# Dividing by the softmax sums with scaled copies on ScalarE in the first two blocks of a fused attention and two-layer kernel

## The chip, the cores and the metric

The kernel runs on one core of a Trainium2 chip. A core has five engines with a queue each: TensorE (PE: matrix products and transposes), VectorE (DVE), ScalarE (ACT), GpSimd (POOL) and SyncE (SP, which here issues the transfers between memory and the core). The metric is the device time of one execution in microseconds; the value given is the median of several runs.

## The reference

For 4 batch items and 8 heads of width 64, each of 512 local queries attends to the keys within 32 positions and to 32 global keys; 32 global queries attend to everything. The result, reordered to 2176 rows of 512, goes through two feed-forward parts.

```python
s_ll = np.where(np.abs(pos[:, None] - pos[None, :]) <= 32, scale * q_l @ k_l.T, -1e9)
s_l = np.concatenate([scale * q_l @ k_g.T, s_ll], axis=-1)
e = np.exp(s_l - max(s_l)); a_l = e / (sum(e) + 1e-09)
out_l = a_l @ concat(v_g, v_l)            # out_g likewise, without the mask
x = concat(out_g, out_l) as (2176, 512)
h = x @ w_in                              # 512 -> 2048
x = where(h > 0, h, exp(min(h, 0)) - 1) @ w_out
xn = x / sqrt(mean(x * x) + 1e-6) * rms_g
out = (silu(xn @ w_gate) * (xn @ w_val)) @ w_o2   # 512 -> 1536 -> 512
```

## The kernel before, in words

The local queries are cut into 16 units of 128 queries, u = 0 to 15, four to a batch item. A unit has all 8 heads, in two halves (`par`) of four. It goes through five helpers. `a_S` makes the scores s of both halves in PSUM on TensorE. `a_E` takes the maximum of each row on VectorE (L227), scales it (L228), and makes the exponentials E on ScalarE, one instruction of 128x128 for each head (L230). `a_T` transposes E on TensorE and copies it out as ET on ScalarE (L238). `a_PV` multiplies by the values; a column of ones among these gives the sum of each row as column 64 of o (L249). `a_N` adds 1e-9 to the sums (L262), inverts them (L263) and multiplies o by the result into x (L264), all on VectorE. `a_X` transposes four units' x and splits them into two parts, xT: a cast on ScalarE (L273) and the rest on VectorE (L274).

Four units make a block of 512 tokens for the first feed-forward part. Block b runs over 16 slices j of the inner width: `mm1` makes h (12 matmuls, L130), `act1` makes the activation tile g in two parts (a cast on ScalarE, L137, and the rest on VectorE, L138), and `mm2` adds g's product to four accumulators y (12 matmuls, L144), one slice later. In block b the units of block b+1 are worked on in between (`att_slot`): scores at j = 0, 4, 8, 12, transposes one slice later, values two slices later.

The weights arrive as raw 64-bit words and are decoded on the way. A tile of 128x1024 takes an absolute value on ScalarE (dx, L81), two one-input passes on VectorE (L88, L89), two two-input passes (L90, L91), a cast on ScalarE (wA, L94) and a subtraction on VectorE (L97). The first layer's 16 tiles are decoded in the prologue (tiles 0 to 2) and in block 0 (one per slice); the last feed-forward part's tiles later.

The prologue (units 0 to 3) has its order written out by hand for TensorE, VectorE and ScalarE (L384 to L433). From block 0 on only TensorE's order is the written one; that of VectorE, ScalarE and SyncE is set by a scheduler at build time, which knows the dependences and its own estimates of durations. Each engine then runs its list strictly in order.

Of the kernel before, what the change touches and what calls it, by code (L numbers as in the profile page):

```python
# [11 lines left out]
AF = mybir.ActivationFunctionType  # L12
ALU = mybir.AluOpType
# [7 lines left out]
P = 128  # L21
# [4 lines left out]
SCALE = 0.125  # L26
# [15 lines left out]
def fused_kernel(ctx: ExitStack, tc: tile.TileContext, kq, vl, gkq, gv, w_in, w_out, w_gate, w_val, w_o2, rms_g, consts, out):  # L42
    nc = tc.nc
# [103 lines left out]
    def new_y():  # L147
        return [yps.tile([P, 512], F32, tag=f"y{i}", name=f"y{i}") for i in range(4)]
# [26 lines left out]
    with ExitStack() as ls:  # L175
# [46 lines left out]
        def a_E(u):  # L222
            ss = s_t.pop(u)
            mx = small.tile([P, 2, 4], F32, tag="st", name="mx")
            e = [ap_.tile([P, 4, P], F32, tag=f"E{par}", name="E") for par in range(2)]
            for par in range(2):
                nc.vector.tensor_reduce(out=mx[:, par, :], in_=ss[par], axis=AX.X, op=ALU.max)  # L227
                nc.vector.tensor_scalar(out=mx[:, par, :], in0=mx[:, par, :], scalar1=-SCALE, scalar2=None, op0=ALU.mult)  # L228
                for pr in range(4):
                    nc.scalar.activation(e[par][:, pr, :], ss[par][:, pr, :], AF.Exp, bias=mx[:, par, pr:pr + 1], scale=SCALE)  # L230
            e_t[u] = e
# [21 lines left out]
        def a_N(u):  # L253
            b, T = u // 4, u % 4
            if T == 0:
                x_t[b] = moe.tile([P, 4, 512], F32, tag="x32", name="x")
            x = x_t[b][:, T, :].rearrange("p (a e d) -> p e a d", a=4, e=2)
            os_ = o_t.pop(u)
            st = small.tile([P, 2, 4, 2], F32, tag="st", name="st")
            for par in range(2):  # L260
                o = os_[par]
                nc.vector.tensor_scalar(out=st[:, par, :, 0:1], in0=o[:, :, 64:65], scalar1=1e-9, scalar2=None, op0=ALU.add)  # L262
                nc.vector.reciprocal(st[:, par, :, 1:2], st[:, par, :, 0:1])  # L263
                nc.vector.tensor_tensor(out=x[:, par], in0=o[:, :, 0:64], in1=st[:, par, :, 1:2].to_broadcast([P, 4, 64]), op=ALU.mult)  # L264

        def a_X(b, cs, xT, pools):

# [11 lines left out]
        def att_slot(b, j, part):  # L279

            u, jj = 4 * (b + 1) + j // 4, j % 4
            if jj == 0 and part == 0:
                a_S(u, ATT2)
                a_E(u)
                load_kq(u + 1)
            if jj == 1 and part == 1:
                a_T(u, 0, aps, "att")
                a_T(u, 1, aps, "att")
            if jj == 2 and part == 0:
                a_PV(u, ATT2)  # L290
                a_N(u)
                load_v(u + 1)
# [91 lines left out]
        with tc.manual_schedule(engines={mybir.EngineType.DVE, mybir.EngineType.Activation}):  # L384
# [11 lines left out]
            a_S(0, ATT2)  # L396
            w1_bits(0)
            a_E(0)
            a_S(1, HB)
            a_T(0, 0, yps, "y0")  # L400
            a_T(0, 1, yps, "y1")
            w1_hi(0)
            a_E(1)
            a_PV(0, Y2)
            w1_lo(0)
            a_N(0)
            w1_abs(1)
            a_S(2, ATT2)
# [3 lines left out]
            w1_bits(1)  # L412
            a_PV(1, Y2)
            a_N(1)
            a_S(3, HB)
            a_T(2, 0, yps, "y0")
# [375 lines left out]
    for k in range(5):  # L792
        n = sizes[k] * P
        xn = xn_t.pop(k)
        os_ = new_y()
# [118 lines left out]
```

## Time and profile before

| what | us |
|---|---|
| median of 3 runs | 933.08 |
| range of the runs | 931.52 to 933.91 |
| profiled execution | 932.09 |
| its span in the profile | 930.0 |
| TensorE busy in the span | 900.3 |
| VectorE busy | 457.9 |
| ScalarE busy | 346.3 |

The span is from the first to the last instruction. Busy times of a whole span are averages over stages: here a prologue, blocks 0 to 3 of the first feed-forward part (block 0 starts at 40.69, block 1 at 150.63, block 2 at 255.17), and the last part. Matmuls overlap, so their rows are longer than the distance from one to the next. The same holds for rows of VectorE and ScalarE: the price of an instruction in a full queue is the distance to the start of the next.

### The profile page before, as it was taken

The numbers are of one execution on the slowest core, as the hardware profiler recorded it, in microseconds if no ns is written. First come the engines' busy times: TensorE is split into PE (matmuls) and PEld (weight loads), VectorE is DVE, ScalarE is ACT, GpSimd is POOL, SyncE is SP. The second block draws the span as 40 slices with busy tenths as digits, with TensorE's granted clock in tenths as the row PEclk, the third lists the DMA queues.
The fourth block names the chain that finished last, engine by engine and source line by source line (L and its number), as shares of the span: only waits on it lengthen the run. The fifth ranks groups of instructions, "written<-read, shape, count | busy, mean of one in ns | idle before, by whom it ended". The sixth has DMA issues, their size and how long they took to land.

```text
span 930.0 us, 15199 instructions
## 1 busy us (share of the span) xinstructions
PE 900.3 (97%) x6482; PEld 752.6 (81%) x6482; DVE 457.9 (49%) x791; ACT 346.3 (37%) x627; POOL 17.9 (2%) x19
## 2 busy tenths in 40 slices
PE   5789999999999999999999999999999999999997
PEld 3567778888878887767888888888889999999996
DVE  4899965676687875443875115221422142142111
ACT  4677754434444433333756113212312232232111
POOL 0000000000000000000101000001000100100000
PEclk8999999999999999999999999999999999999999
DMA  9686443455576743532644001100100010000000
GB/s 360 268 300 214 158 178 123 166 181 195 213 275 219 281 160 137 176 137 90 228 126 144 1 1 35 45 1 1 35 20 27 1 34 35 1 1 35 1 1 35
DMA packets 34443, 107.74 MB, mean 116 GB/s; under 512 B 3016, under 2 KB 5704, under 8 KB 31816
## 3 DMA queue, kind: packets, MB, share of 16 engines
q1 hardware_dynamic: 34376, 106.77, 32.2%
q8 instruction: 51, 0.84, 0.4%
q14 instruction: 16, 0.13, 0.0%
HBM read 88.41 MB, written 18.35 MB: 115 GB/s over the span
## 4 chain that ended last, share of the span: by engine, by line
PE 87%; DVE 7%; issue 2%; DMA 2%; ACT 2%; SPq 0%; ACTq 0%; DVEq 0%
PE y L144 17%; PE h L130 16%; PE pg L631 15%; PE pv L631 15%; PE y L637 15%; PE o L249 2%; DVE dx L90 1%; PE ptp L236 1%; PE yg L595 1%; PE hg L579 1%; PE s L218 1%; DVE dx L91 1%; DVE wA L97 1%; DMA raw<-in_moe_w_in 1%; DVE dx L88 1%
## 5 line engine op out<-in xcount | busy, mean ns | idle before, releaser
L144 PE MATMUL y<-g,wA 128*128 128x512 f32 x768 | 199.0, 402 | 6.3 <-DVE g L138 4.5
L130 PE MATMUL h<-xT,wA 128*128 128x512 f32 x768 | 186.4, 392 | 1.3 <-DVE xT L274 1.3
L144 PEld LDWEIGHTS y<-g,wA 128*128 128x128 f32 x768 | 140.7, 190 | 42.4 <-DVE g L138 6.4
L130 PEld LDWEIGHTS h<-xT,wA 128*128 128x128 f32 x768 | 144.0, 189 | 32.3 <-DVE xT L274 1.5
L804 DVE TENSOR_TENSOR silu<-pv,silu 128x384 f32<-128x384 f32 (+1 forms) x60 | 36.6, 611 | 257.2 <-PE pv L631 251.2
L637 PE MATMUL y<-wB,p 128*128 128x512 f32 x612 | 149.0, 391 | 0.0
L637 PEld LDWEIGHTS y<-wB,p 128*128 128x128 f32 x612 | 114.4, 188 | 22.4
L803 ACT ACTIVATE silu<-pg 128x384 f32<-128x384 f32 (+1 forms) x60 | 32.1, 534 | 159.5 <-PE pg L631 159.4
L631 PE MATMUL pv<-xT,wB 128*128 128x384 f32 (+1 forms) x432 | 88.4, 352 | 0.0
L631 PEld LDWEIGHTS pv<-xT,wB 128*128 128x128 f32 x432 | 77.3, 188 | 5.6
L806 ACT CAST p<-silu 128x384 fp32r<-128x384 f32 (+1 forms) x60 | 33.3, 555 | 127.0 <-DVE silu L804 126.8
L137 ACT CAST g<-e 128x512 fp32r<-128x512 f32 x64 | 39.7, 621 | 64.9 <-DVE e L113 61.1
L111 ACT ACTIVATE e<-h 128x512 f32<-128x512 f32 x48 | 28.9, 602 | 92.5 <-PE h L130 86.6
L631 PE MATMUL pv<-xnB,wB 128*128 128x512 f32 (+1 forms) x288 | 61.5, 362 | 0.0
L631 PE MATMUL pg<-xT,wB 128*128 128x384 f32 (+1 forms) x288 | 60.0, 357 | 0.0
L631 PEld LDWEIGHTS pg<-xT,wB 128*128 128x128 f32 x288 | 52.2, 188 | 5.8 <-issue 0.5
L631 PEld LDWEIGHTS pv<-xnB,wB 128*128 128x128 f32 x288 | 52.2, 188 | 5.6
L807 DVE TENSOR_TENSOR p<-silu,p 128x384 fp32r<-128x384 f32 (+1 forms) x60 | 38.0, 633 | 35.5 <-ACT p L806 35.5
L112 DVE TENSOR_SCALAR e<-e 128x512 f32<-128x512 f32 x52 | 22.2, 427 | 64.6 <-ACT e L111 64.3
L138 DVE TENSOR_TENSOR g<-e,g 128x512 fp32r<-128x512 f32 x64 | 45.0, 703 | 15.3 <-ACT g L137 14.4
L81 ACT ACTIVATE dx<-raw 128x1024 f32<-128x1024 f32 x34 | 39.1, 1151 | 12.3 <-DVE wA L97 6.1
L90 DVE SCALAR_TENSOR_TENSOR dx<-raw,dx 128x1024 int32<-128x1024 int32 x34 | 42.0, 1239 | 0.6
(153 smaller groups left out, 911.1 us busy)
## 6 DMA issues: line engine op xcount, KB each, us to landing
raw<-in_moe_w_out SPq DMA_DIRECT2D x14, 1024.0 KB, 5.7
wT<-dx SPq DMA_DIRECT2D x18, 512.0 KB, 3.3
wraw<-wT SPq DMA_DIRECT2D x18, 512.0 KB, 4.4
raw<-in_moe_w_in SPq DMA_DIRECT2D x8, 1024.0 KB, 8.7
raw<-in_moe_w_gate SPq DMA_DIRECT2D x6, 1024.0 KB, 6.4
raw<-in_moe_w_val SPq DMA_DIRECT2D x6, 1024.0 KB, 6.9
gvr<-in_gv SPq DMA_DIRECT2D x8, 640.0 KB, 4.8
gkq<-in_gkq SPq DMA_DIRECT2D x4, 1152.0 KB, 5.2
```

The source lines that it names most:

```text
L81: ins = nc.scalar.activation(x, f(words(raw)[:, :, 1]), AF.Abs)
L90: nc.vector.scalar_tensor_tensor(out=i32(x), in0=word[:, :, 1], scalar=-0x40000000, in1=i32(x), op0=ALU.bitwise_and, op1=ALU.bitwise_or)
L130: nc.tensor.matmul(h[:, :n], W1[c, G][:, ws, o:o + P], xT[c][:, xs, :n], start=(k == 0), stop=(k == 11))
L137: nc.scalar.copy(g[:, 0, :n], e[:, :n])
L138: nc.vector.tensor_tensor(out=g[:, 1, :n], in0=e[:, :n], in1=f(g[:, 0, :n]), op=ALU.subtract)
L144: nc.tensor.matmul(ys[dc][:, :n], W2[j][:, ws, dc * P:(dc + 1) * P], g[:, gs, :n], start=(j == 0 and k == 0), stop=(j == 15 and k == 2))
L631: nc.tensor.matmul(ps[:, :n], W[c, G3][:, ws, o:o + P], xn[c][:, xs, :n], start=(k == 0), stop=(k == 11))
L637: nc.tensor.matmul(os_[t], p[:, pp, t * P:(t + 1) * P], Wo[j][:, ww, :], start=(j == 0 and k == 0), stop=(j == 11 and k == 2))
L803: nc.scalar.activation(s[:, :n], pg[:, :n], AF.Silu)
L804: nc.vector.tensor_tensor(out=s[:, :n], in0=pv[:, :n], in1=s[:, :n], op=ALU.mult)
L806: nc.scalar.copy(p[:, 0, :n], s[:, :n])
L807: nc.vector.tensor_tensor(out=p[:, 1, :n], in0=s[:, :n], in1=f(p[:, 0, :n]), op=ALU.subtract)
```

## The change

In `a_E` the maxima of both halves are scaled by one instruction on 128x8, after both reductions, instead of by one on 128x4 after each. In `a_N` the reciprocals of both halves are joined in the same way. For units 0 to 7 (the prologue's four, and the four that are worked on in block 0) the product on VectorE is replaced by eight copies on ScalarE, one for each head, of 128x64, with the reciprocal as the per-partition scale.

```diff
             for par in range(2):
                 nc.vector.tensor_reduce(out=mx[:, par, :], in_=ss[par], axis=AX.X, op=ALU.max)
-                nc.vector.tensor_scalar(out=mx[:, par, :], in0=mx[:, par, :], scalar1=-SCALE, scalar2=None, op0=ALU.mult)
+            nc.vector.tensor_scalar(out=mx, in0=mx, scalar1=-SCALE, scalar2=None, op0=ALU.mult)
+            for par in range(2):
                 for pr in range(4):
                     nc.scalar.activation(e[par][:, pr, :], ss[par][:, pr, :], AF.Exp, bias=mx[:, par, pr:pr + 1], scale=SCALE)
...
             for par in range(2):
+                nc.vector.tensor_scalar(out=st[:, par, :, 0:1], in0=os_[par][:, :, 64:65], scalar1=1e-9, scalar2=None, op0=ALU.add)
+            nc.vector.reciprocal(st[:, :, :, 1:2], st[:, :, :, 0:1])
+            for par in range(2):
                 o = os_[par]
-                nc.vector.tensor_scalar(out=st[:, par, :, 0:1], in0=o[:, :, 64:65], scalar1=1e-9, scalar2=None, op0=ALU.add)
-                nc.vector.reciprocal(st[:, par, :, 1:2], st[:, par, :, 0:1])
-                nc.vector.tensor_tensor(out=x[:, par], in0=o[:, :, 0:64], in1=st[:, par, :, 1:2].to_broadcast([P, 4, 64]), op=ALU.mult)
+                if u < 8:
+                    for pr in range(4):
+                        nc.scalar.activation(x[:, par, pr], o[:, pr, 0:64], AF.Copy, scale=st[:, par, pr, 1:2])
+                else:
+                    nc.vector.tensor_tensor(out=x[:, par], in0=o[:, :, 0:64], in1=st[:, par, :, 1:2].to_broadcast([P, 4, 64]), op=ALU.mult)
```

ScalarE's list in the prologue, from the exponentials of unit 1 to the ET copies of unit 3, before:

```order
L230 ACTIVATE E<-s,mx 128x128 x8
L81 ACTIVATE dx<-raw 128x1024
L238 COPY ET<-ptp 128x512 x2
L230 ACTIVATE E<-s,mx 128x128 x8
L238 COPY ET<-ptp 128x512 x2
L230 ACTIVATE E<-s,mx 128x128 x8
L94 CAST wA<-dx 128x2x512
L238 COPY ET<-ptp 128x512 x2
```

The same place on ScalarE in the changed kernel, whose line numbers are up to six higher:

```order
L231 ACTIVATE E<-s,mx 128x128 x8
L268 ACTIVATE x<-o,st 128x64 x8
L81 ACTIVATE dx<-raw 128x1024
L239 COPY ET<-ptp 128x512 x2
L231 ACTIVATE E<-s,mx 128x128 x8
L268 ACTIVATE x<-o,st 128x64 x8
L239 COPY ET<-ptp 128x512 x2
L231 ACTIVATE E<-s,mx 128x128 x8
L94 CAST wA<-dx 128x2x512
L268 ACTIVATE x<-o,st 128x64 x8
L239 COPY ET<-ptp 128x512 x2
```

The copies of unit 0 now stand ahead of tile 1's absolute value, those of unit 1 ahead of unit 2's ET copies, and those of unit 2 ahead of unit 3's.

VectorE's list in block 0 from the ninth g to the tenth, before (numbers tell apart tiles of one name):

```order
L138 TENSOR_TENSOR g_1203<-e_1199,g_1203 128x512
L228 TENSOR_SCALAR mx_1242<-mx_1242 128x4
L90 SCALAR_TENSOR_TENSOR dx_1328<-raw_1055,dx_1328 128x1024
L88 TENSOR_SCALAR dx_1412<-dx_1412 128x1024
L91 SCALAR_TENSOR_TENSOR dx_1328<-raw_1055,dx_1328 128x1024
L89 TENSOR_SCALAR dx_1412<-dx_1412 128x1024
L90 SCALAR_TENSOR_TENSOR dx_1412<-raw_1141,dx_1412 128x1024
L121 SCALAR_TENSOR_TENSOR e_1295<-e_1295,h_1282 128x512
L91 SCALAR_TENSOR_TENSOR dx_1412<-raw_1141,dx_1412 128x1024
L97 TENSOR_TENSOR wA_1334<-dx_1328,wA_1334 128x2x512
L138 TENSOR_TENSOR g_1299<-e_1295,g_1299 128x512
```

And in the changed kernel, again from the ninth g to the tenth:

```order
L138 TENSOR_TENSOR g_1227<-e_1223,g_1227 128x512
L228 TENSOR_SCALAR mx_1266<-mx_1266 128x8
L97 TENSOR_TENSOR wA_1446<-dx_1440,wA_1446 128x2x512
L89 TENSOR_SCALAR dx_1481<-dx_1481 128x1024
L90 SCALAR_TENSOR_TENSOR dx_1481<-raw_1208,dx_1481 128x1024
L91 SCALAR_TENSOR_TENSOR dx_1481<-raw_1208,dx_1481 128x1024
L88 TENSOR_SCALAR dx_1574<-dx_1574 128x1024
L121 SCALAR_TENSOR_TENSOR e_1318<-e_1318,h_1305 128x512
L89 TENSOR_SCALAR dx_1574<-dx_1574 128x1024
L97 TENSOR_TENSOR wA_1487<-dx_1481,wA_1487 128x2x512
L90 SCALAR_TENSOR_TENSOR dx_1574<-raw_1303,dx_1574 128x1024
L138 TENSOR_TENSOR g_1322<-e_1318,g_1322 128x512
```

Between these two g there are two subtractions wA now, where one stood before. Of the 14 such subtractions that follow the last xT part of the prologue (tiles 2 to 15), 13 stand ahead of the tenth g now, and 11 did before.

## Rows read from the trace of the kernel before

**Rows 1.** Busy us by stage: stretch, length, engines (instructions), TensorE clock, DMA share, GB/s.

```profile
0.00:40.69 40.69, 24.43 (x568) 17.97 (x569) 23.71 (x55) 22.54 (x53) 0.20 (x4) 0.87 0.90 357
40.69:113.58 72.89, 68.39 (x606) 53.86 (x610) 72.56 (x103) 49.95 (x84) 0.00 (x0) 0.98 0.59 204
113.58:150.63 37.05, 36.87 (x351) 30.07 (x339) 24.32 (x45) 19.90 (x37) 0.00 (x0) 1.00 0.46 163
150.63:255.17 104.54, 104.54 (x954) 85.32 (x952) 67.16 (x123) 42.65 (x86) 0.00 (x0) 1.00 0.52 185
255.17:362.00 106.83, 104.61 (x943) 84.80 (x942) 78.76 (x138) 44.59 (x86) 0.00 (x0) 0.98 0.64 227
```

**Rows 2.** Timeline of ScalarE, prologue: start, length, what, [wait before <-releaser].

```profile
16.12 2.18 ACT L230 ACTIVATE E<-s,mx 128x128 f32<-128x128 f32 x8 [4.88 <-DVE mx L228]
...
22.30 1.21 ACT L81 ACTIVATE dx<-raw 128x1024 f32<-128x1024 f32 x1
23.34 1.14 ACT L238 COPY ET<-ptp 128x512 f32<-128x512 f32 x2
24.28 2.27 ACT L230 ACTIVATE E<-s,mx 128x128 f32<-128x128 f32 x8
29.10 1.08 ACT L238 COPY ET<-ptp 128x512 f32<-128x512 f32 x2 [2.55 <-PE ptp L236]
30.96 2.17 ACT L230 ACTIVATE E<-s,mx 128x128 f32<-128x128 f32 x8 [0.79 <-DVE mx L228]
32.98 1.09 ACT L94 CAST wA<-dx 128x1024 fp32r<-128x1024 f32 x1
34.21 1.18 ACT L238 COPY ET<-ptp 128x512 f32<-128x512 f32 x2
...
38.13 2.05 ACT L273 CAST xT<-xtp 128x512 fp32r<-128x512 f32 x4 [1.67 <-PE xtp L272]
```

**Rows 3.** Timeline of VectorE, prologue.

```profile
15.93 0.69 DVE L227 TENSOR_REDUCE mx<-s 128x4 f32<-128x512 f32 x1
16.64 0.17 DVE L228 TENSOR_SCALAR mx<-mx 128x4 f32<-128x4 f32 x1
...
24.64 0.69 DVE L88 TENSOR_SCALAR dx<-dx 128x1024 f32<-128x1024 f32 x1
...
28.49 0.16 DVE L262 TENSOR_SCALAR st<-o 128x4 f32<-128x4 f32 x1
```

**Rows 4.** Timeline of TensorE, end of the prologue.

```profile
33.27 0.32 PE L249 MATMUL o<-v,ET 128*32 128x65 f32 x6 [2.39 <-issue]
...
40.69 3.00 PE L130 MATMUL h<-xT,wA 128*128 128x512 f32 x12 [1.28 <-DVE xT L274]
```

**Rows 5.** Timeline of VectorE, block 0, from the tenth g.

```profile
113.58 0.69 DVE L138 TENSOR_TENSOR g<-e,g 128x512 fp32r<-128x512 f32 x1
114.18 1.22 DVE L97 TENSOR_TENSOR wA<-dx,wA 128x1024 fp32r<-128x1024 f32 x1
115.32 0.22 DVE L262 TENSOR_SCALAR st<-o 128x4 f32<-128x4 f32 x2
115.46 0.68 DVE L88 TENSOR_SCALAR dx<-dx 128x1024 f32<-128x1024 f32 x1
116.06 0.23 DVE L263 RECIPROCAL st<-st 128x4 f32<-128x4 f32 x2
116.21 0.66 DVE L121 SCALAR_TENSOR_TENSOR e<-e,h 128x512 f32<-128x512 f32 x1
...
117.39 0.75 DVE L264 TENSOR_TENSOR x<-o,st 128x256 f32<-128x256 f32 x2
118.05 1.21 DVE L90 SCALAR_TENSOR_TENSOR dx<-raw,dx 128x1024 int32<-128x1024 int32 x1
119.18 0.68 DVE L88 TENSOR_SCALAR dx<-dx 128x1024 f32<-128x1024 f32 x1
```

**Rows 6.** Timeline of TensorE, block 0, the step that uses the tenth g.

```profile
114.39 3.00 PE L144 MATMUL y<-g,wA 128*128 128x512 f32 x12
```

## The prediction

> **What bounds the kernel now.** I read the busy table by stage first, then ScalarE's and VectorE's timelines of the prologue, then VectorE's timeline in block 0. The table [rows 1] shows three kinds of stage. In block 1 TensorE is busy for 104.54 of 104.54 us: nothing that other engines do there can shorten it. In the prologue (0 to 40.69 us) TensorE works 24.43 of 40.69 us, so this stage is a chain of small steps over three engines. From 40.69 to 113.58 us VectorE works 72.56 of 72.89 us and TensorE 68.39: VectorE, which decodes the weights, sets the pace together with TensorE. So the change can only count in the prologue and in the first two thirds of block 0, and both must be priced.
>
> The prologue's chain runs along ScalarE. In [rows 2] one instruction follows another from 16.12 to 26.5 us without a wait; after that the only waits are 2.55, 0.79 and 1.67 us, the last just ahead of the xT casts. The first matmul of block 0 starts at 40.69 and had waited for VectorE's xT parts, which follow those casts [rows 4].
>
> **What the change adds to the prologue.** Per unit, ScalarE gets eight copies of 128x64 out of PSUM, with the reciprocal as scale; VectorE loses two 128x256 products, one reciprocal and one scaling. ScalarE's order there is written by hand, so eight copies stand ahead of named instructions: after the second unit's exponentials and before the absolute value of weight tile 1, and so on.
>
> The trace has no 128x64 copy. Nearest are the eight 128x128 exponentials, also from PSUM with a per-partition operand: 30.96 to 32.98 is 0.2525 us each, start to start. Two 128x512 copies take 0.94, 0.47 each (23.34 to 24.28) [rows 2]. A line through both gives (0.47 - 0.2525) / 384 = 0.00057 us a column, so 0.2525 - 64 x 0.00057 = 0.216 at 64 columns; I take 0.21, which is 1.7 us a unit. Bounds: half an exponential (cost by columns alone), 1.0 us; a whole exponential, 2.0 us; eight that do not overlap, at the single length 2.17 - 7 x 0.2525 = 0.40, 3.2 us.
>
> The row for back-to-back exponentials is 0.2525 us [rows 2]. The Trainium skill (ScalarE: Activation LUTs, What ACT_TABLE_LOAD costs) gives an instruction with a pointer operand 280 ns plus 0.833 ns a column and lets neighbours overlap by 93 ns, which would be 0.294 us here; the measurement is lower and decides. By that page 64 columns would be 0.24 us, 1.9 a unit, an estimate, and the sum below would rise by 0.8 us.
>
> Now the chain, step by step.
> 1. The first exponential started at 16.12, once the first half's maxima were scaled. With one scaling for both halves it waits for the second reduction too, which ends at 15.93 + 0.69 = 16.62, and for a scaling of 0.17 [rows 2, 3]: 16.8, so +0.7.
> 2. Copies of unit 0: +1.7. The absolute value of tile 1 moves from 22.30 to 24.7 and ends 1.2 us later at 25.9.
> 3. VectorE's four decode steps of tile 1, from 24.64 to 28.49, wait for it and begin at 25.95: +1.3. Behind them on VectorE stand unit 1's sums (28.49 to 29.8) [rows 3]; two sums and one reciprocal make 30.25. This is a wait that before had no cost: the copies of unit 1 cannot start until 30.25, and unit 2's ET copies stand behind them on ScalarE. They start at 31.95 instead of 29.10: +2.85.
> 4. Unit 3's exponentials follow 0.94 later, at 32.9 against 30.96: +1.95, because the wait of 0.79 is gone. TensorE's stop of 2.39 us before 33.27, where the profile names no engine, lies beside this and does not end last any more [rows 4]. Then 2.0 us of exponentials, about 1.0 for wA and 1.7 for unit 2's copies: unit 3's ET copies at 37.6 against 34.21, +3.4.
> 5. Unit 3's own division: one product of 0.42 and a transpose stood between its last reciprocal and the casts; now eight copies, 1.7, with the transposes beside them, less what the joined reciprocal saves. I take +0.5.
>
> Prologue: 3.4 + 0.5 = **+3.9 us**. All four sets of copies lie on this path, so 0.1 us a unit moves it by about 0.4: 1.0 us a unit gives +1.1, 2.0 gives +5.1, 3.2 gives +9.9.
>
> **What it moves in block 0.** TensorE's order is the same word for word. VectorE's is not: it is left to a scheduler, which sorted it anew. A second-layer step on TensorE needs both parts of an activation tile g, and the second part is VectorE's. I counted what stands on VectorE between the last xT part and the tenth g. Before: 24 passes of the one-input kind over a weight tile, 24 of the two-input kind, 11 wA subtractions, 4 products x, 6 scalings, 4 reciprocals. After: 28, 27, 13, none, 3, 2. The remaining kinds are equal in number (10 e, 10 g, 6 reductions, 4 sums). So the saved time is there, but decoding has been pulled ahead of the tenth g.
>
> Prices, start to start [rows 5]: one-input pass 0.60 (115.46 to 116.06), two-input pass 1.13 (118.05 to 119.18), wA 1.14 (114.18 to 115.32), two products 0.66 (117.39 to 118.05), two reciprocals 0.15; a scaling has the same shape as a sum, two of which take 0.14. Added: 4 x 0.60 + 3 x 1.13 + 2 x 1.14 = 8.1. Removed: 4 x 0.33 + 3 x 0.07 + 2 x 0.075 = 1.7. The tenth g comes **6.4 us** later, counted from the end of the prologue. The cover for this is thin: before, the tenth g started at 113.58 and was done at 114.27 [rows 5], while TensorE entered the step that uses it at 114.39 and needs the second part with its second matmul [rows 6], so about 0.4 us is absorbed. VectorE had no gap to give (0.33 us idle in 72.89) [rows 1].
>
> Behind the tenth g the new order has less decoding left: by the sixteenth g it is ahead by 3.3 us of work. That does not come back, because from there TensorE is the bound: it was busy 36.87 of 37.05 us to the end of block 0 [rows 1] and has the same instructions.
>
> Blocks 1 and 2 lose three small VectorE instructions a unit. In block 1 they lie under a full TensorE: nothing. In block 2 TensorE lacks 2.2 us of 106.83 [rows 1]; the change touches the order there slightly, and I book nothing, with 1 us either way.
>
> **Sum.** 3.9 + 6.4 - 0.4 = +9.9 us. The profiled execution took 932.09 (span 930.0 and 2.1 around it), so 942.0; the median of the timed runs lies 1.0 above that execution, so **943.0 us**.
>
> **Rivals.**
> A, faster. VectorE is the full engine in block 0, and it is relieved by 0.8 us a unit, 3.3 by the sixteenth g. If the copies cost 1.0 us a unit or less, four sets are 4 us against 5.0 us of ScalarE's waits (2.55 + 0.79 + 1.67), and the prologue could hide them; if then the decoding that was pulled ahead stands where VectorE would have waited, the relief of the first two units (1.7) to all four (3.3) comes through: 933.1 less 1.7 to 3.3, about 930.5. For it: VectorE 72.56 of 72.89 busy [rows 1]. Against: the counts up to the tenth g, and that the waits of 2.55 and 1.67 lie behind steps which themselves move. It decides from a copy price of 0.125 us down. The Trainium skill (Perfetto Trace Analysis, Optimizing Scalar/DVE Operations) says that with a saturated VectorE moving work to ScalarE may make sense; by that rule this rival is the expected one, and the trace agrees on the saturation but not on ScalarE being free in the prologue.
>
> B, prologue only. If VectorE's order in block 0 does not bind (TensorE has been late by the prologue's delay and the g come in time after all), only +3.9 remains: 937.0. For it: TensorE is nearly as full as VectorE there. Against: the prologue's delay moves VectorE's start by as much as TensorE's.
>
> C, dearer copies. Small instructions that do not overlap, 0.40 us each: the prologue +9.9, the total +15.9, 949. For it: the copies write a tile with gaps between its pieces; against: the exponentials overlap.
>
> D, no change: the copies hide as in A and the order costs what the relief gives: 933.
>
> **Chances.** Forecast (940 to 946.5) 0.65; B, or in between, 0.13; C 0.12; A 0.05; D 0.05. About 0.3%, 2.8 us, is what a measurement of this kernel can tell from no change. Faster 0.05, same 0.05, slower 0.90. The range that takes in B and the lower part of C is 936.5 to 946.5; the forecast's own range is 940 to 946.5, by copies of 1.0 to 2.0 us a unit (940.2 to 944.2) with room for longer waits.
>
> **What would show it.** In the new profile: eight copies in about 1.7 us; the first exponential near 16.8; unit 2's ET copies near 32 and unit 3's near 37.6; block 0's first h matmul near 44.6; the tenth g near 123.9 with TensorE waiting for VectorE at several g between the sixth and the tenth; then equal lengths of blocks 1 and 2. It is wrong if h starts before 42, if TensorE shows no wait for g in 85 to 125 us, or if block 1 changes its length.

## The result, and the profile after

The changed kernel took **943.4 us** (median of 6 runs, 941.41 to 945.95), against 931.5 (930.17 to 933.91) before in the same comparison: a ratio of **1.0126, 95% interval 1.0114 to 1.0138**, so 1.3% slower. The forecast was 943.0 in a range of 936.5 to 946.5. The profiled execution took 941.41 us with a span of 939.6, which is 9.6 more than the span of before.

The head of the page of the changed kernel: ScalarE has 64 instructions more than the 627 of before (eight copies in each of eight units), VectorE 48 fewer than its 791, and neither is near the span. The totals do not show where 9.6 us went.

```profile
span 939.6 us, 15209 instructions
PE 903.1 (96%) x6482; PEld 754.3 (80%) x6482; DVE 450.4 (48%) x743; ACT 359.0 (38%) x691; POOL 17.9 (2%) x19
```

Busy time by stage of the changed kernel, with the columns of [rows 1] and cut at the same events: first matmul of block 0, tenth g, first matmul of block 1, of block 2, end of block 2; and a last row for a stretch in block 0 of which more is said below.

```profile
0.00:43.05 43.05, 24.18 (x568) 17.79 (x568) 19.45 (x39) 28.80 (x85) 0.20 (x4) 0.88 0.85 337
43.05:124.04 80.99, 72.78 (x655) 56.67 (x655) 79.89 (x104) 57.45 (x104) 0.00 (x0) 0.94 0.58 209
124.04:160.40 36.36, 35.59 (x286) 29.25 (x287) 14.94 (x29) 19.18 (x47) 0.00 (x0) 1.00 0.32 110
160.40:264.99 104.59, 104.59 (x954) 85.30 (x952) 66.83 (x115) 42.75 (x86) 0.00 (x0) 1.00 0.52 185
264.99:371.80 106.81, 104.70 (x945) 84.90 (x944) 78.23 (x130) 44.34 (x87) 0.00 (x0) 0.98 0.63 227
...
94.40:100.00 5.60, 5.52 (x13) 4.36 (x14) 5.60 (x8) 2.87 (x9) 0.00 (x0) 0.50 0.45 140
```

Read against [rows 1], the lengths say where the time went: prologue 40.69 to 43.05, **+2.36**; first matmul of block 0 to the tenth g 72.89 to 80.99, **+8.10**; from there to block 1, 37.05 to 36.36, -0.69; block 1 +0.05 and block 2 -0.02; the rest of the span 568.0 to 567.8. The sum is 9.6. Nearly all of the loss lies in the first two thirds of block 0, where VectorE is busy for 79.89 of 80.99 us.

ScalarE's timeline of the changed prologue answers to [rows 2]. L268 are the copies, eight to a row.

```profile
15.76 2.17 ACT L231 ACTIVATE E<-s,mx 128x128 f32<-128x128 f32 x8 [5.48 <-DVE mx L228]
...
21.93 1.80 ACT L268 ACTIVATE x<-o,st 128x64 f32<-128x64 f32 x8
23.50 1.24 ACT L81 ACTIVATE dx<-raw 128x1024 f32<-128x1024 f32 x1
...
29.25 1.75 ACT L268 ACTIVATE x<-o,st 128x64 f32<-128x64 f32 x8 [1.47 <-DVE st L263]
30.84 1.13 ACT L239 COPY ET<-ptp 128x512 f32<-128x512 f32 x2
...
34.72 1.89 ACT L268 ACTIVATE x<-o,st 128x64 f32<-128x64 f32 x8
36.30 1.28 ACT L239 COPY ET<-ptp 128x512 f32<-128x512 f32 x2
...
38.86 1.75 ACT L268 ACTIVATE x<-o,st 128x64 f32<-128x64 f32 x8 [0.16 <-PE xtp L278]
```

Eight copies take 1.57 to 1.59 us from their start to the next instruction's (21.93 to 23.50, 29.25 to 30.84, 34.72 to 36.30), 0.197 each. The wait of 1.47 ahead of unit 1's copies is the new one: they wait for the joined reciprocal, which stands on VectorE behind the decoding of tile 1. The gap between two units' ET copies, which was 5.11 (29.10 to 34.21), is 5.46 (30.84 to 36.30).

VectorE in block 0 up to the tenth g, answering to [rows 5]:

```profile
116.45 0.69 DVE L89 TENSOR_SCALAR dx<-dx 128x1024 int32<-128x1024 int32 x1
117.17 1.23 DVE L90 SCALAR_TENSOR_TENSOR dx<-raw,dx 128x1024 int32<-128x1024 int32 x1
118.43 1.22 DVE L91 SCALAR_TENSOR_TENSOR dx<-raw,dx 128x1024 int32<-128x1024 int32 x1
...
122.90 1.26 DVE L90 SCALAR_TENSOR_TENSOR dx<-raw,dx 128x1024 int32<-128x1024 int32 x1
124.04 0.72 DVE L138 TENSOR_TENSOR g<-e,g 128x512 fp32r<-128x512 f32 x1
```

The tenth g starts at 124.04, and what stands before it is decoding for tiles that TensorE needs only later. TensorE at the sixth g and at the tenth, which answers to [rows 6], shows who paid:

```profile
91.93 0.50 PE L144 MATMUL y<-g,wA 128*128 128x512 f32 x1 [1.09 <-ACT g L137]
94.48 5.06 PE L144 MATMUL y<-g,wA 128*128 128x512 f32 x11 [2.06 <-DVE g L138]
99.34 3.42 PE L130 MATMUL h<-xT,wA 128*128 128x512 f32 x12
...
123.33 0.50 PE L144 MATMUL y<-g,wA 128*128 128x512 f32 x1
124.81 2.81 PE L144 MATMUL y<-g,wA 128*128 128x512 f32 x11 [0.98 <-DVE g L138]
```

One matmul of a step goes ahead with the first part of g, and the other eleven wait for VectorE's part: 2.06 us at the sixth g and 0.98 at the tenth. In before the tenth step ran without a stop [rows 6], and so did the sixth:

```profile
87.92 3.22 PE L144 MATMUL y<-g,wA 128*128 128x512 f32 x12
```

All of block 0, before and after, by engine:

```profile
40.69:150.63 109.94, 105.26 (x941) 83.93 (x941) 96.88 (x147) 69.84 (x119) 0.00 (x0) 0.98 0.55 190
43.05:160.40 117.35, 108.37 (x941) 85.92 (x942) 94.83 (x131) 76.63 (x151) 0.00 (x0) 0.96 0.50 178
```

The block is 7.4 us longer on TensorE: it stands idle for 4.3 us more (8.98 against 4.68), and the same matmuls take 3.1 us more, at a lower granted clock.

### The profile page after: what moved, and what is told of

It is laid out like the page before. It is cut to its first block, busy times and chain, and to the rows that moved or that the text cites. A ratio compares the mean times of both kernels' runs of the same rounds, so it can differ in the third digit from the quotient of the medians.

```text
span 939.6 us, 15209 instructions
## 1 busy us (share of the span) xinstructions
PE 903.1 (96%) x6482; PEld 754.3 (80%) x6482; DVE 450.4 (48%) x743; ACT 359.0 (38%) x691; POOL 17.9 (2%) x19
## 4 chain that ended last, share of the span: by engine, by line
PE 87%; DVE 6%; DMA 3%; ACT 2%; issue 1%; SPq 0%; ACTq 0%; DVEq 0%
PE y L144 17%; PE h L130 16%; PE pg L637 15%; PE pv L637 15%; PE y L643 15%; DVE dx L90 2%; PE o L250 1%; PE ptp L237 1%; PE yg L601 1%; PE hg L585 1%; DMA raw<-in_moe_w_out 1%; PE s L218 1%; DVE dx L91 1%; DMA yT<-yev 1%; ACT x L268 1%
## 5 line engine op out<-in xcount | busy, mean ns | idle before, releaser
L81 ACT ACTIVATE dx<-raw 128x1024 f32<-128x1024 f32 x34 | 39.7, 1168 | 12.4 <-DVE wA L97 5.6
L231 ACT ACTIVATE E<-s,mx 128x128 f32<-128x128 f32 x128 | 35.0, 399 | 19.7 <-DVE mx L228 19.7
```

The source lines that it names most:

```text
L81: ins = nc.scalar.activation(x, f(words(raw)[:, :, 1]), AF.Abs)
```

## The experiments

The changed kernel differs from before in three ways: the copies of units 0 to 3 in the prologue, the copies of units 4 to 7 in block 0, and the joined scalings and reciprocals. And VectorE's list in block 0 comes out in another order. Two theories were set against each other. By **the list**, block 0 is lengthened by the order that the scheduler gives VectorE and ScalarE, above all VectorE, whichever part of the edit led to it, and the copies cost some 2 to 3 us in the prologue only. By **the copies**, the time comes from the instructions themselves, so that it goes when they go.

The first four kernels take the parts singly. `join_only` keeps the joins and drops all copies (the product on VectorE stays):

```diff
-                if u < 8:
+                if 0 <= u < 0:
```

> The two joined instructions alone; all products stay on VectorE, no copies on ScalarE. List theory (the loss in block 0 comes from the order of VectorE's list, which the scheduler sorted anew): the work on VectorE from the last xT part to the tenth g, summed at the durations of the kernel before, is 79.5 us against 72.8 before and 79.2 in the changed kernel, so the shift comes with the joining alone. Prologue +0.4 us (the first exponential waits for both reductions), block 0 about +9 to 10, since here VectorE is not relieved: 941 us, ratio to before 1.008 to 1.012. Copy theory (the copies on ScalarE are the cost in both stages): without copies nothing is left but 0.4 us, 932, ratio 1.000 to 1.001.

`copies_0_3_only` is the kernel before with copies in the prologue and nothing joined:

```diff
-                nc.vector.tensor_tensor(out=x[:, par], in0=o[:, :, 0:64], in1=st[:, par, :, 1:2].to_broadcast([P, 4, 64]), op=ALU.mult)
+                if 0 <= u < 4:
+                    for pr in range(4):
+                        nc.scalar.activation(x[:, par, pr], o[:, pr, 0:64], AF.Copy, scale=st[:, par, pr, 1:2])
+                else:
+                    nc.vector.tensor_tensor(...)
```

> Copies on ScalarE for units 0 to 3 alone (the prologue's), nothing joined. List theory: prologue +1.8 us (less than the change's, since the first exponential and unit 1's reciprocals aren't held up by a join), and VectorE's list in block 0 is again another one: 76.3 us of work up to the tenth g against 72.8, so about +4 in block 0 although none of its units has copies: 937 us, ratio 1.005 to 1.008. Copy theory: the prologue's share of the copies, +2 to +3, and block 0 as long as before: 934, ratio 1.002 to 1.003.

`join_copies_4_7` is the changed kernel without the prologue's copies:

```diff
-                if u < 8:
+                if 4 <= u < 8:
```

> Everything joined, copies for units 4 to 7 alone (block 0's); the prologue's products stay on VectorE. List theory: prologue +0.4 as with the joining alone; block 0 as in the changed kernel, +7, since VectorE's list is that of the changed kernel there (79.2 us to the tenth g): 938.5 us, ratio 1.006 to 1.009; shorter than the joining alone by 2 to 3 us, because these copies do relieve VectorE. Copy theory: longer than the joining alone by what ScalarE pays for four sets of copies, some 6 us: it must be the slower of the two.

`change_order_before` has the changed kernel's instructions, all of them, but VectorE's and ScalarE's order in block 0 is written by hand, as a list of small steps that follows the order of before. The hand-written order of the prologue is kept open through the block:

```diff
-        with tc.manual_schedule(engines={mybir.EngineType.DVE, mybir.EngineType.Activation}):
+        hand = ExitStack()
+        hand.enter_context(tc.manual_schedule(engines={mybir.EngineType.DVE, mybir.EngineType.Activation}))
...
-        moe_block(0, slot0)
+        block0()
+        hand.close()
```

Here `block0()` walks the list (h and y are TensorE's two steps, b88 to b91 the decoding passes of lines 88 to 91, ghi and glo the two parts of g, and so on) and issues each step in its place.

> The changed kernel with all its instructions, joined and with eight sets of copies, but in block 0 VectorE and ScalarE are written out by hand in the order of the kernel before (each joined instruction at the place of the second of its pair, the copies where the products stood in time). TensorE's order is unchanged. List theory: prologue as in the changed kernel, +3; in block 0 the work to the tenth g falls to 71.0 us, and block 0 is about 1 us longer or shorter than before: 935 us, ratio 1.002 to 1.006, about 6 to 8 us faster than the changed kernel. Copy theory: the instructions are the same, so is the time: 943, ratio 1.011 to 1.014.

Four more followed. `before_order_by_hand` has the instructions of before, and block 0 in a written order of my own in which less decoding stands ahead of each g; `change_order_by_hand` does the same with the changed kernel's instructions, `copies_4_7_order_by_hand` with copies for units 4 to 7 alone, joined reciprocals and separate scalings. The first lines of the first list:

```diff
+        BLOCK0 = """
+            abs:3 h:0 b88:2 b88:3 b89:2 b89:3 e1:0 b90:2 S:4 e2:0 b90:3 h:1 b91:2 e3:0 hi:2 red4.0 ghi:0 lo:2 e1:1 e2:1 glo:0 abs:4 mx4.0 red4.1 y0a
...
```

> The kernel before, with no instruction changed, but block 0's order on VectorE and ScalarE written by hand: each e, maximum and g as soon as TensorE can use it, and the decoding of a weight tile in the gaps, about one slice ahead of its use. Work on VectorE up to the tenth g 65.8 us against 72.8 in the scheduler's order. List theory: the first y step starts 1 to 2 us sooner and TensorE hardly waits for g after it, block 0 shorter by 4 to 5.5 us: 926 to 928 us, ratio 0.994 to 0.996. Rival (VectorE is full, so the work and not its order sets block 0): the same work, the same time, 931.5, ratio 0.999 to 1.001.

> The changed kernel with all its instructions, and block 0's order written by hand in the same manner: 67.0 us of work to the tenth g against 79.2. List theory: the prologue keeps its +3, block 0 gets shorter by about 12 us than in the changed kernel: 929 to 932 us, so level with the kernel before, ratio 0.997 to 1.001. Rival (the work sets block 0): 943, ratio 1.012.

> Copies for units 4 to 7 alone, reciprocals joined, maxima scaled separately, block 0's order by hand (64.4 us to the tenth g). The prologue is that of the kernel before but for the joined reciprocals (+0.4 us at most). List theory: as the kernel before with the order by hand, 0 to 1 us less, because VectorE has 0.7 us less to do for each of the four units while TensorE is the bound through most of block 0: 925 to 928, ratio 0.993 to 0.996. Copy theory: four sets of copies on ScalarE, 6 us, show at least in part: above the kernel before with the order by hand by 3 us or more.

`copies_0_7_nothing_joined` is `copies_0_3_only` with `0 <= u < 8`, in the scheduler's order.

> All eight sets of copies, nothing joined, the scheduler's order. List theory: prologue +2 to +2.7 as with the copies of units 0 to 3 alone; VectorE's list has 78.5 us of work to the tenth g, so block 0 +6 to +7: 939 to 941, ratio 1.008 to 1.011, slower than the copies of units 0 to 3 alone although VectorE is relieved of four more units' products. Copy theory: also slower than with the copies of units 0 to 3 alone, by about 3, 940. The two are told apart in the trace: by the list theory TensorE's waits in block 0 name VectorE's g, by the copy theory ScalarE's g or ET.

**What was measured.** Ratios are to before on the same chip, with their 95% interval. "First h" is the start of block 0, "block 0" its length to the first matmul of block 1, both from the profiled execution. "Work" is what stands on VectorE between the first h and the tenth g, counted by kinds and priced with the start-to-start times of before ([rows 5] and its like).

| kernel | median us | ratio (95%) | first h | block 0 | work |
|---|---|---|---|---|---|
| before | 931.5, 932.1 | 1 | 40.69 | 109.94 | 72.8 |
| changed kernel | 943.4 | 1.0126 (1.0114 to 1.0138) | 43.05 | 117.35 | 79.2 |
| join_only | 944.8 | 1.0140 (1.0122 to 1.0159) | 40.73 | 120.93 | 79.5 |
| copies_0_3_only | 937.7 | 1.0067 (1.0047 to 1.0086) | 43.38 | 114.22 | 76.3 |
| join_copies_4_7 | 940.3 | 1.0089 (1.0057 to 1.0122) | 40.67 | 119.31 | 79.2 |
| copies_0_7_nothing_joined | 941.2 | 1.0108 (1.0087 to 1.0129) | 43.56 | 117.90 | 78.5 |
| change_order_before | 936.9 | 1.0054 (1.0037 to 1.0071) | 45.19 | 111.27 | 71.0 |
| before_order_by_hand | 926.3 | 0.9945 (0.9928 to 0.9961) | 40.88 | 105.24 | 65.8 |
| change_order_by_hand | 932.2 | 0.9997 (0.9983 to 1.0011) | 44.80 | 108.80 | 67.0 |
| copies_4_7_order_by_hand | 927.0 | 0.9955 (0.9938 to 0.9973) | 40.77 | 105.15 | 64.4 |

**The copies fall, the list stands.** `join_only` has not one copy on ScalarE and *fewer* instructions on VectorE than before, and it lost no less than the changed kernel did (the two intervals overlap). That is more than the list theory had expected of it, 1.008 to 1.012. Its prologue is as long as that of before, and its block 0 is the longest of all. Its stage row up to the tenth g, and its matmuls at the sixth:

```profile
40.73:123.75 83.02, 73.06 (x655) 57.30 (x655) 79.92 (x109) 54.52 (x88) 0.00 (x0) 0.92 0.59 206
```

```profile
90.14 0.50 PE L144 MATMUL y<-g,wA 128*128 128x512 f32 x1 [1.09 <-ACT g L137]
92.69 4.63 PE L144 MATMUL y<-g,wA 128*128 128x512 f32 x10 [2.05 <-DVE g L138]
```

The same stop stands at the same step, 1.09 and 2.05 us. The joining alone brings the scheduler to the late order (79.5 us of work ahead of the tenth g against 72.8). It is not the joining in particular, though: `copies_0_7_nothing_joined` joins nothing, carries 78.5 us ahead of the tenth g and has a block 0 of 117.90. Two different edits led to late lists, and a smaller one, `copies_0_3_only`, to one between (76.3 us, 114.22).

The counted work is not all of it. `join_copies_4_7` has VectorE's instructions of block 0 in the order of the changed kernel, kind by kind, the same 79.2 us of work, and yet a block 0 of 119.31 against 117.35: up to the tenth g VectorE stood idle for 3.1 us there, in `join_only` too, against 1.1 in the changed kernel and 0.3 before. The longest of its waits in both (1.03 and 1.52 us) is for a tile whose raw words were still on their way: the decoding had been pulled ahead of them. In the four kernels with late lists ScalarE's absolute value (L81) waited 2.5 to 4.5 us for such words up to the tenth g; in the others no such wait is marked. The longest of these waits stands in `copies_0_7_nothing_joined`, where it holds up the exponentials behind it on ScalarE, and these hold up TensorE:

```profile
114.86 1.13 ACT L81 ACTIVATE dx<-raw 128x1024 f32<-128x1024 f32 x1 [4.24 <-DMA raw<-in_moe_w_out]
115.90 2.15 ACT L230 ACTIVATE E<-s,mx 128x128 f32<-128x128 f32 x8
117.07 0.66 PE L236 MATMUL ptp<-ident,E 128*128 128x128 f32 x4 [1.49 <-ACT E L230]
```

So what was expected of this kernel's waits came out split: in its block 0 TensorE waited 3.8 us for VectorE's g (3.5 in before) and 2.8 for ScalarE's E (0.6 in before). These rows put the longest wait for E down to the order of ScalarE's list and to the loads, and not to a copy.

The same instructions, ordered otherwise, settle it between the two theories: from the changed kernel to `change_order_before` only the order around block 0 differs (the decoding of tile 2 goes from the prologue's list into the block's with it), and the time falls from 943.4 to 936.9. With a better list it falls to 932.2, all copies and joins in place. The written orders fix ScalarE's list as well as VectorE's, so these runs show that the order decides, and not how much of it is VectorE's alone. And `before_order_by_hand` shows that the list of before was not a good one either: 65.8 us of work ahead of the tenth g, a block 0 shorter by 4.7 us, and a kernel that beats both, at 0.9945. Its block 0 by engine, and TensorE's longest waits there (us in total, times, longest):

```profile
40.88:146.12 105.24, 103.06 (x940) 82.97 (x941) 98.26 (x146) 70.21 (x119) 0.00 (x0) 1.00 0.54 190
```

```profile
PE y L144 <- DVE g L506: 0.8, 1, 0.8
PE ptp L588 <- ACT E L581: 0.8, 2, 0.4
PE y L144 <- ACT g L502: 0.5, 1, 0.5
```

Against them the waits for g in block 0 of before (the first row) and of the changed kernel, in the same columns:

```profile
PE y L144 <- DVE g L138: 3.5, 3, 2.6
PE y L144 <- DVE g L138: 5.6, 3, 2.6
PE y L144 <- ACT g L137: 2.7, 2, 1.6
```

TensorE waited 3.5 us for VectorE's parts of g in before and 5.6 in the changed kernel; with the written order it is 0.8. In the first two cases 2.6 of it is the wait at the first g. TensorE's granted clock is 1.00 throughout with the written order (0.94 in the changed kernel to the tenth g, 0.98 in before).

**What each set of copies is worth.** In the prologue: every kernel without copies there starts block 0 at 40.67 to 40.88, joined or not, every kernel with them at 43.05 to 45.19. So it is the copies that cost the +2.4 us and more. The joins show no cost where no copies stand. They hold the first exponential up by 0.6 us, but every kernel without copies in the prologue has a stop of TensorE further on, of 1.2 to 2.5 us and with no engine named (the one of [rows 4]). The 0.6 us may be lost in it: in these five kernels the first exponential starts at 15.25 to 16.21, and block 0 within 0.21 us of one another. In `join_only` the stop is this row:

```profile
32.74 0.32 PE L250 MATMUL o<-v,ET 128*32 128x65 f32 x6 [2.36 <-issue]
```

Whether the joins cost anything behind the copies is not shown: in `copies_0_3_only` and `copies_0_7_nothing_joined`, which would tell, the granted clock was 0.54 and 0.55 over the last transposes of the prologue, against 1.00 in the changed kernel. The two latest starts, 44.80 and 45.19, have the clock in them too: it was 0.50 there. The row of `change_order_before` from 38 to 50 us, and its first step of block 0:

```profile
38.00:50.00 12.00, 10.54 (x91) 8.55 (x92) 7.30 (x13) 6.50 (x15) 0.00 (x0) 0.50 0.22 88
```

```profile
45.19 5.24 PE L130 MATMUL h<-xT,wA 128*128 128x512 f32 x12 [0.55 <-DVE xT L280]
```

Twelve matmuls took 5.24 us instead of 3.00 [rows 4]. That is 2.2 us in block 0 besides the later start, so these two traces hold a cost of the clock besides those of the list and the copies. For `change_order_by_hand` the profiled execution, 935.1 us at a mean clock of 0.986, was the slowest of ten; the two with the highest mean clock, 0.995 and 0.997, took 929.8 and 928.3. Why the clock was low there in these kernels, and 1.00 in the changed kernel, was not tried.

In block 0 the copies of units 4 to 7 are no burden: `join_copies_4_7` differs from `join_only` by them alone in its source, and its span is 2.2 us shorter (938.7 against 940.9). But the scheduler ordered block 0 differently in the two, and the two intervals just touch at 1.0122, so a relief is possible and not shown. With a written order there is nothing left of it: 0.9955 with these copies, 0.9945 without, intervals on top of each other.

## Why the prediction was right

**The number.** That 943.4 came so near to 943.0 is in part luck. The forecast was +9.9 us on a median of 933.1; in the comparison that was measured the median of before is 931.5, so the change cost 11.9 us, 2.0 more than forecast. The trace read here is of the fastest of the changed kernel's six executions, 941.41 us, 9.3 above the profiled one of before; what the other executions lost besides is not in it.

**Prologue: mechanism right, term too large.** Forecast +3.9, measured +2.36. Three pieces of the difference can be read. The first exponential started at 15.76, not 16.8. It did wait for both halves: ScalarE stood still ahead of it for 5.48 us, against 4.88 in before, and the same 5.48 shows in `join_only` and `join_copies_4_7`, 4.88 in the kernels that join nothing. But the step of TensorE that waits for the second load of keys and queries began earlier in this execution, 13.45 against 14.35:

```profile
13.45 1.16 PE L218 MATMUL s<-kq 64*32 64x128 f32 x64 [2.06 <-DMA kq<-in_kq]
```

In the other profiled executions this row starts anywhere from 13.39 to 14.12, with and without the edits, so the 0.9 us are not the change's, and with the later start the prologue would, by estimate, have come nearer to the forecast. The copies cost 1.58 us a unit, not 1.7. And steps 3 and 4, taken from the first exponential on, come out at 15.1 (30.84) and 20.5 us (36.30) after it, where the forecast had 15.15 and 20.8; so the chain was drawn rightly, with unit 1's copies behind the decoding as its new wait. The last step, booked at +0.5, took +0.27 (36.30 to 43.05 against 34.21 to 40.69). In sum the start accounts for 1.04 of the 1.5 us that were forecast too much, the chain for 0.26 and the last step for 0.23. The experiments confirm that this term goes with the copies and stands apart from block 0.

**Block 0: mechanism right, term too small.** Forecast +6.4 up to the tenth g, from counted instructions; measured +8.1. The two errors, 1.5 too much and 1.7 too little, cancelled, and the tenth g fell at 124.04 where 123.9 was forecast: that agreement is better than the working deserves. The rows name nearly all of the 1.7, by the distance from each instruction to the next against the prices used. Three waits of VectorE of 0.17 to 0.19 us are marked, with what they lose of the overlap 0.9 us; before had one, 0.3 us. Instructions that take their neighbour's result cost more than the prices: 117.17 to 118.43 is 1.26 for a pass whose price was 1.13, and 116.45 to 117.17 is 0.72 for one of 0.60. There are six such rows in the new list against three, 0.4 us more. And at four places VectorE came to a result of ScalarE that was only just done, a gap too short for the profile to mark as a wait. One of them, VectorE's two rows and ScalarE's between them:

```profile
120.93 0.69 DVE L89 TENSOR_SCALAR dx<-dx 128x1024 int32<-128x1024 int32 x1
120.66 1.06 ACT L94 CAST wA<-dx 128x1024 fp32r<-128x1024 f32 x1
121.75 1.23 DVE L97 TENSOR_TENSOR wA<-dx,wA 128x1024 fp32r<-128x1024 f32 x1
```

ScalarE's cast ends at 121.72, and 120.93 to 121.75 is 0.82 for a pass of 0.60. The four places (from 100.16, 115.08, 119.57 and 120.93) make 0.7 us. So the step that was too small is the price: the count took every instruction as independent of its neighbours and of ScalarE.

**What followed.** The slack at the tenth g was booked at -0.4; the stage behind it came out 0.69 shorter. Blocks 1 and 2 kept their lengths within 0.05 us, so what VectorE saves under a full TensorE was worth nothing, as stated (they lose two small VectorE instructions a unit, not three: 123 to 115 and 138 to 130 in the tables). The waits of TensorE for VectorE between the sixth g and the tenth are at these two g alone, 3.0 us in all, and not at several; at the sixth TensorE also waited 1.09 us for ScalarE's part. The forecast did not have the fall of TensorE's clock behind the sixth.

**The rivals.** A (faster) fell on its price, 0.197 us a copy where it needed 0.125, and on the order: `join_copies_4_7`, without a copy in the prologue, is slower than before as well. The rule that stood beside A in the Trainium skill (Perfetto Trace Analysis, Optimizing Scalar/DVE Operations), that with VectorE saturated moving work to ScalarE may make sense, found no gain here: with the order written, the copies of units 4 to 7 give 0.9955 against 0.9945 without them, and there TensorE, busy for 102.97 of the 105.15 us of block 0, is the bound. B (prologue only) fell with block 0's +8.1. C (dearer copies, 0.40 each) fell by the same 0.197. D fell with the sum.

**Where the working was thinner than the result.** The prediction took the new order as a fact of the change and counted it, which is why it came out right. It did not say which part of the edit led to it, and a reader could take it for the price of the copies. The runs say otherwise: 2.4 us go with the copies, and the rest with lists that the scheduler sorted anew, which it also did when only two small instructions a unit were joined. It also took VectorE's work alone: that decoding ahead of its time can wait for its words from memory, and that TensorE's clock falls behind a stop, stand in no term of the sum.

## What to carry to other kernels

Where a scheduler sorts an engine's list, any edit, even one that only removes instructions, may give another list. So compare the lists, count the work that stands ahead of each item that the next engine waits for, and price that, before the instructions of the edit themselves. Add what it would have to wait for: here the decoding that was pulled ahead met tiles that had not landed. If the count moves a nearly full engine's critical item, write that stretch's order by hand and measure the edit again: here the order was worth 11 us (943.4 against 932.2, the same instructions), and with written orders the edit's instructions cost 6 (932.2 against 926.3), in the prologue and, in part, by a lower clock of TensorE at the start of block 0. A join saves an instruction, but makes the first consumer wait for the last producer, by 0.6 us at the first exponential here.

## What had not been expected of the hardware

TensorE's granted clock fell behind some of its stops. After the two waits of 1.09 and 2.06 us at the sixth g it was 0.50 (1.2 of 2.4 GHz) from 94.4 to 100 us: eleven matmuls took 5.06 us and the next twelve 3.42, against 2.81 for eleven at 124.81. VectorE was busy for all of these 5.6 us, and for 46.04 of the 46.53 us from 77.51 to the tenth g, for which TensorE then still waited 0.98; so up to there the slow clock lay beside VectorE's list and need not have cost more. But at the start of block 0 in `change_order_before` nothing hid it, and one step was 2.2 us longer. The written order of `before_order_by_hand`, in which TensorE hardly stops, has 1.00 in all of block 0.

Back-to-back copies of 128x64 out of PSUM, each with its own scale from memory, cost 0.197 us start to start, only 0.055 less than exponentials of twice the columns (0.2525, [rows 2]). By these two rows, which differ in the function too, most of the price of so small an instruction does not depend on its columns. The Trainium skill (ScalarE: Activation LUTs, What ACT_TABLE_LOAD costs) led to an estimate of 0.24 in the prediction; the measurement is lower and decides.
